# A linear-attention and ELU kernel: one batch's attention cut by heads in place of rows, and two weight matmul blocks moved ahead of a late operand

## The chip, the cores and the metric

The kernel runs on one core of one Trainium2 chip. The metric is device time in microseconds (us) of one execution; a profile's span is about 2 us shorter than that time, because it counts from the first to the last instruction. With one core there is no second die to compare with; every profiled run quoted here is at a granted TensorE clock of 0.997 to 1.0.

PE is TensorE's matrix unit (PEld its weight loads), DVE is VectorE, ACT is ScalarE, POOL is GpSimd, SP is SyncE. PSUM is the memory that PE's products go to; in these kernels a product that reuses a PSUM buffer waits until the buffer's last reader is through. A turn is a transpose on PE. An insertion is a group of small attention matmuls (64 rows) put between the full-size matmuls of a layer.

## The reference

The attention is linear (no softmax), its output is RMS-normed per head, and a two-layer network with ELU follows:

```python
# q, k, v: (8 batches, 8 heads, 576 rows, 64); w_in: 512 x 2048; w_out: 2048 x 512
kv  = einsum('bhsd,bhse->bhde', k, v)          # 64 x 64 per head, over all 576 rows
out = einsum('bhsd,bhde->bhse', q, kv)         # "scores" in the kernel
rms = sqrt(mean(out*out, axis=-1) + 1e-6)
x   = (out / rms * g_norm) -> (4608 tokens, 512)
h   = x @ w_in                                 # first layer
g   = where(h > 0, h, exp(min(h, 0)) - 1)      # ELU
y   = g @ w_out                                # second layer, float32
```

## The kernel before

The kernel works in groups T of 512 rows: group T is batch T's first 512 rows, and a ninth group collects the remaining 64 rows of all batches. The first layer has 16 output blocks f of 128 columns, done as pairs i (f = 2i, 2i+1). Each needs four matmuls, one per 128-row block c of `w_in`; a column block c of x is two heads. The second layer of a group has four output tiles j, each a sum over the 16 blocks f. The batch's attention is put between matmuls of the previous group's second layer, so that DVE and ACT work while PE goes on. PSUM has three pools that matter here: `at` (one buffer), `m1` (two buffers of two banks), `m2` (two buffers of one bank).

The three places that the change touches, in the order of time. First, the weights come in four slices, and batch 0's first six blocks f wait for one late column block of x (c = 3):

```python
edges = (0, 512, 1024, 1536, 2048)             # columns of w_in, one load per slice
...
first((0, 1, 2, 3), (0,))                      # first(fs, cs): blocks fs, rows cs
mean_first(3); log_first(3); exp_first(3); scale_first(3)    # makes x's block c = 3
first((0, 1, 2, 3), (1, 2))
for f in (0, 1, 2, 3):
    first((f,), (3,))
for f in (4, 5):
    first((f,), (0, 1, 2, 3))
... # ELU of pair 0 reads PSUM twice (exp on ACT, max on DVE), of pair 1 on ACT only
for i, parts in enumerate([[(0, 2, pair)]] + single):
    elu(0, i, parts, i == 1)()
```

Second, batch 1's attention inside batch 0's second layer. `q` turns Q, `kv` is K·V for all heads, `se` the scores, `sq`, `sum`, `inv`, `mul` the norm, and `x0`, `x1` turn x by halves of the rows:

```python
order = (2, 3, 0, 1)
for j in order: mm2_quarter(0, j, 0)           # second layer, f 0-3
at["q"]()
for j in order: mm2_quarter(0, j, 1)           # f 4-7
mm2(0, order[0], 8, 10)
at["kv"]()                                     # all 8 heads: needs the last K and V slices
for j in order[1:]: mm2(0, j, 8, 10)
at["se"]({0: None, 1: ps_m1.tile(...)})        # all heads; row half 0 in "at", 1 in "m1"
... sq0, sq1, sum0, inv0, sum1, inv1, mul0, mul1
for j in order: mm2(0, j, 10, 12)
for j in order:
    mm2(0, j, 12, FC, hold=j in (2, 3))
    ...
    if j == 0: at["x0"]()                      # turn of rows 0-255, scaled copy on ACT
```

Third, batch 1's first products, in two row halves, so that they can start with half of x; `x1` comes between:

```python
firsts = [ps_m1.tile(...) for _ in range(2)]
for cs in (slice(0, 256), slice(256, G)):
    for f in range(4):
        for c in range(KC):
            nc.tensor.matmul(firsts[f // 2][:, f % 2, cs], lhsT=w_in_sb[:, c, f*P : f*P+P],
                             rhs=xT[1](c, cs), start=(c == 0), stop=(c == KC - 1))
        if cs.start == 0 and f == 1: head_x1()  # turn of rows 256-511, scaled copy on DVE
```

## Time and profile before

The first three runs had a median of 285.66 us (285.45 to 285.68). The six that the result was compared with had 285.56 us.

| what | before |
|---|---|
| span of the profile | 283.7 us |
| PE busy | 274.4 us, 97% |
| DVE, ACT busy | 56%, 54% |
| idle PE listed by the waits | 3.7 us, of which 2.4 at start-up, all but traces of it before 47 us |

The first part of the page gives each engine's busy time, its share and its instructions:

```profile
PE 274.4 (97%) x2131; PEld 130.5 (46%) x2162; DVE 159.9 (56%) x231; ACT 153.1 (54%) x220; POOL 53.5 (19%) x94
```

PE is the bottleneck, so a gain has to come from its gaps or its work. The Trainium skill ("Trainium Kernel Development and Optimization", Performance Expectations) warns that matmul busy time is a poor measure of how close a kernel is to the limit, because matmuls are pipelined; gaps must be read from the spacing of starts, and the page's 97% hides them. PE's waits (what waited, for what, total us, times, longest):

```profile
PE bank L547 <- DVE q_two L150: 1.2, 2, 0.8
PE h_ps L607 <- DVE xT L598: 0.4, 1, 0.4
PE h_ps L802 <- ACT xT L312: 0.4, 1, 0.4
```

The first is start-up. The other two are the ones the change is about. The timeline of PE (start, duration, line, operation, count, and the recorded idle before it) shows where they stand, from batch 0's first product (14.37) to K·V of batch 2 (54.37); a full-width matmul starts every 0.216 us:

```profile
14.37 0.61 PE L607 MATMUL h_ps<-xT,w_in_sb 128*128 128x512 bf16 x2
...
16.82 0.59 PE L607 MATMUL bank<-xT,w_in_sb 128*128 128x512 bf16 x2
17.85 0.59 PE L607 MATMUL h_ps<-xT,w_in_sb 128*128 128x512 bf16 x2 [0.43 <-DVE xT L598]
...
29.07 1.24 PE L445 MATMUL o_ps<-w_out_sb,gT 128*128 128x512 bf16 x5
...
40.30 4.49 PE L445 MATMUL o_ps<-w_out_sb,gT 128*128 128x512 bf16 x19
44.83 0.62 PE L305 MATMUL at<-ident,xs 128*128 128x128 bf16 x8
45.29 1.03 PE L445 MATMUL o_ps<-w_out_sb,gT 128*128 128x512 bf16 x4
46.69 1.03 PE L802 MATMUL h_ps<-xT,w_in_sb 128*128 128x256 bf16 x8 [0.37 <-ACT xT L312]
47.55 0.61 PE L305 MATMUL at<-ident,xs 128*128 128x128 bf16 x8
48.00 2.99 PE L802 MATMUL h_ps<-xT,w_in_sb 128*128 128x256 bf16 x24
...
54.37 0.78 PE L174 MATMUL at<-v_pk,k_pk 64*64 64x64 bf16 x72
```

The two matmuls at 16.82 should be followed at 17.25; the next starts at 17.85, so 0.6 us is lost, more than the recorded 0.43, because a matmul's modelled end overlaps the next start. In the same way the four matmuls at 45.29 should be followed at 46.15, and 0.54 us is lost before 46.69. The turn at 44.83 is 0.2 us late (20 matmuls from 40.30 end at 44.62; one record is missing), and the second row half waits 0.22 us inside the line at 48.00 (the weight loads have that gap at 49.08). The three around the turn come to 0.96 us.

The chain that ended last (start, us, what) confirms that this stretch is bound by the norm on DVE and ACT, not by PE:

```profile
40.18 1.03 ACT sq L213
...
41.23 0.95 DVE ss L218
...
42.37 1.22 DVE ss L218
...
43.61 0.32 ACT ss L224
...
44.17 1.45 ACT o_sb L458 x3
45.62 1.02 ACT xT L312
...
46.69 1.03 PE h_ps L802 x8
```

Three copies of output tiles (`o_sb`) stand in this chain ahead of ACT's x copy, and the change moves them behind it.

### The profile page before, as it was taken

The numbers are of one execution on the slowest core, as the hardware profiler recorded it, in microseconds if no ns is written. First come the engines' busy times: TensorE is split into PE (matmuls) and PEld (weight loads), VectorE is DVE, ScalarE is ACT, GpSimd is POOL, SyncE is SP. The second block draws the span as 40 slices with busy tenths as digits, with TensorE's granted clock in tenths as the row PEclk, the third lists the DMA queues.
The fourth block names the chain that finished last, engine by engine and source line by source line (L and its number), as shares of the span: only waits on it lengthen the run. The fifth ranks groups of instructions, "written<-read, shape, count | busy, mean of one in ns | idle before, by whom it ended". The sixth has DMA issues, their size and how long they took to land.

```text
span 283.7 us, 5180 instructions
## 1 busy us (share of the span) xinstructions
PE 274.4 (97%) x2131; PEld 130.5 (46%) x2162; DVE 159.9 (56%) x231; ACT 153.1 (54%) x220; POOL 53.5 (19%) x94
## 2 busy tenths in 40 slices
PE   6999999999999999999999999999999999999994
PEld 2444555545544444445444444444444444444443
DVE  2359315698478636934695468544864486444400
ACT  2779535766496338634773378246923692333311
POOL 7823402251421060104210421012000000000000
PEclk9999999999999999999999999999999999999999
DMA  7999999796993598356944794355253123010122
GB/s 194 204 207 202 207 201 178 225 143 113 196 190 68 150 134 181 76 148 90 208 95 127 105 213 94 98 130 148 49 93 83 77 48 100 2 74 0 74 75 75
DMA packets 55979, 35.99 MB, mean 127 GB/s; under 512 B 32788, under 2 KB 53524, under 8 KB 55956
## 3 DMA queue, kind: packets, MB, share of 16 engines
q0 software_dynamic: 20208, 17.30, 39.7%
q1 hardware_dynamic: 35348, 17.83, 23.6%
q10 hardware_dynamic: 400, 0.52, 0.5%
q8 instruction: 17, 0.28, 0.4%
q14 instruction: 6, 0.05, 0.0%
HBM read 36.70 MB, written 9.44 MB: 163 GB/s over the span
## 4 chain that ended last, share of the span: by engine, by line
PE 90%; ACT 3%; DVE 3%; DMA 2%; issue 1%; SPq 0%
PE h_ps L398 39%; PE o_ps L445 36%; PE o_ps L858 5%; DMA st_q<-in_q_dram 2%; PE at L174 2%; PE h_ps L802 1%; DVE ss L218 1%; PE at L201 1%; PE bank L607 1%; ACT sq L213 1%; PE at L398 1%; PE bank L577 1%; PE bank L529 1%; ACT o_sb L458 1%; PE se_ps L201 1%
## 5 line engine op out<-in xcount | busy, mean ns | idle before, releaser
L398 PE MATMUL h_ps<-xT,w_in_sb 128*128 128x512 bf16 x524 | 123.6, 380 | 0.2
L445 PE MATMUL o_ps<-w_out_sb,gT 128*128 128x512 bf16 x488 | 117.9, 379 | 1.4 <-issue 0.3
L410 ACT ACTIVATE elu_e<-h_ps 128x1024 bf16<-128x1024 f32 (+1 forms) x72 | 70.8, 991 | 83.8 <-PE h_ps L398 79.2
L398 PEld LDWEIGHTS <-w_in_sb 128*128 128x128 bf16 x536 | 50.8, 98 | 61.5 <-DVE xT L333 1.7
L445 PEld LDWEIGHTS <-gT 128*128 128x128 bf16 x512 | 49.6, 98 | 59.1
L421 DVE TENSOR_SCALAR elu_e<-elu_e 128x1024 bf16<-128x1024 bf16 (+1 forms) x75 | 32.3, 431 | 70.5 <-ACT elu_e L410 70.5
L429 DVE TENSOR_TENSOR gT<-elu_e,h_ps 128x1024 bf16<-128x1024 bf16 (+1 forms) x53 | 62.6, 1181 | 5.9 <-DVE elu_e L421 0.5
L218 DVE TENSOR_REDUCE ss<-sq 128x16 f32<-128x1024 bf16 x16 | 19.3, 1218 | 13.4 <-ACT sq L213 12.7
L458 ACT COPY o_sb<-o_ps 128x512 f32<-128x512 f32 x32 | 18.5, 585 | 14.4 <-PE o_ps L445 14.4
L150 POOL COPY q_bf<-q_pk 128x512 bf16<-128x512 bf16 x24 | 14.6, 636 | 23.5 <-DMA q_pk<-in_q_dram 23.5
L416 ACT ACTIVATE elu_h<-h_ps 128x1024 bf16<-128x1024 f32 (+1 forms) x19 | 18.3, 968 | 0.0
L429 DVE TENSOR_TENSOR gT<-elu_e,elu_h 128x1024 bf16<-128x1024 bf16 x19 | 13.2, 693 | 2.9 <-ACT elu_h L416 1.7
L858 PE MATMUL o_ps<-w_out_sb,gT 128*128 128x512 bf16 (+1 forms) x79 | 14.0, 336 | 0.1
L125 POOL COPY gate<-qT 1x1 bf16<-1x1 bf16 x6 | 1.1, 179 | 59.9 <-DMA qT<-q_bf 59.9
L229 DVE TENSOR_TENSOR xs<-at,ss 128x512 bf16<-128x512 f32 x18 | 11.5, 682 | 1.2 <-ACT ss L225 1.2
L104 POOL DMA_DIRECT2D q_pk<-in_q_dram x14 | 10.5, 759 | 4.7 <-issue 1.9
L213 ACT ACTIVATE sq<-at 128x1024 bf16<-128x1024 f32 x9 | 9.4, 1044 | 2.4 <-PE at L201 2.4
L858 PEld LDWEIGHTS <-gT 128*128 128x128 bf16 x80 | 7.7, 98 | 6.4 <-DVE gT L429 0.4
L118 POOL DMA_DIRECT2D v_pk<-in_v_dram x12 | 8.4, 702 | 5.0 <-DMA w_in_sb<-in_moe_w_in_dram 2.9
L118 POOL DMA_DIRECT2D k_pk<-in_k_dram x12 | 8.3, 694 | 5.1 <-DMA w_in_sb<-in_moe_w_in_dram 3.4
L866 ACT COPY o_last<-o_ps 128x512 f32<-128x512 f32 (+1 forms) x5 | 2.5, 500 | 10.8 <-PE o_ps L858 10.8
L529 PE MATMUL bank<-zeros 128*128 128x512 bf16 x19 | 6.6, 465 | 1.4 <-DVE zeros L506 1.2
(73 smaller groups left out, 138.6 us busy)
## 6 DMA issues: line engine op xcount, KB each, us to landing
out_dram<-o_sb SPq DMA_DIRECT2D x16, 512.0 KB, 3.0
q_pk<-in_q_dram POOLq DMA_DIRECT2D x14, 256.0 KB, 5.0
k_pk<-in_k_dram POOLq DMA_DIRECT2D x6, 576.0 KB, 8.1
v_pk<-in_v_dram POOLq DMA_DIRECT2D x6, 576.0 KB, 12.2
w_in_sb<-in_moe_w_in_dram POOLq DMA_DIRECT2D x4, 512.0 KB, 10.9
w_out_sb<-in_moe_w_out_dram POOLq DMA_DIRECT2D x3, 512.0 KB, 15.5
st_q<-in_q_dram SPq DMA_DIRECT2D x2, 512.0 KB, 4.7
st_q<-in_q_dram SPq DMA_DIRECT2D x16, 64.0 KB, 2.5
```

Of the source, the lines that this page charges most:

```text
L118: nc.gpsimd.dma_start(out=raw[name, b].rearrange("p h j d -> p h (j d)")[:, hs], in_=in_[:, hs])
L150: eng.tensor_copy(out=out_, in_=in_)
L213: nc.scalar.activation(sq, se_ps, AF.Square)
L218: nc.vector.reduce_sum(out=ss, in_=sq.rearrange("p c (h e) -> p (c h) e", h=H), axis=AX.X)
L398: nc.tensor.matmul(h_ps[a][:, cs], lhsT=w_in_sb[:, c, f * P : f * P + P], rhs=x(c, cs), start=(c == 0), stop=(c == KC - 1),)
L410: nc.scalar.activation(e[:, lo:hi, :], ps, AF.Exp)
L416: nc.scalar.activation(h[:, lo:hi, :], ps, AF.Relu)
L421: nc.vector.tensor_scalar(out=e[:, lo:hi, :], in0=e[:, lo:hi, :], scalar1=1.0, scalar2=1.0, op0=ALU.min, op1=ALU.subtract,)
L429: nc.vector.tensor_tensor(out=gT[T][:, 2 * i + lo : 2 * i + hi, :], in0=e[:, lo:hi, :], in1=h, op=ALU.add if relu else ALU.max,)
L445: nc.tensor.matmul(o_ps[T, j], lhsT=gT[T][:, f, j * P : j * P + P], rhs=w_out_sb[:, f, :], start=(f == 0), stop=(f == FC - 1),)
L458: nc.scalar.copy(o_sb[T][:, j % 2, :], o_ps.pop((T, j)))
L858: nc.tensor.matmul(ps, lhsT=gT[B][:, f, j * P : j * P + P], rhs=w_out_sb[:, f, cols], start=(f == 0), stop=(f == FC - 1),)
```

## The change

The intent: start batch 1's norm earlier by doing half of the heads as soon as the first halves of K and V are there, so that x is ready when PE asks; and fill batch 0's gap with blocks f 4 and 5, for which the second `w_in` slice is made narrower. The core of the diff (the new pieces `kvu`, `seu`, `mulu`, `xu` do for heads of pair index u what `kv`, `se`, `mul`, `x` did for all heads or a row half; their bodies are cut):

```diff
-    edges = (0, 512, 1024, 1536, 2048)
+    edges = (0, 512, 768, 1280, 1664, 2048)
...
-    for f in (0, 1, 2, 3):
-        first((f,), (3,))
-    for f in (4, 5):
-        first((f,), (0, 1, 2, 3))
+    first((4, 5), (0, 1, 2))
+    first((0, 1, 2, 3, 4, 5), (3,))
...
-    (the order of batch 1's attention shown above)
+    scores = ps_m1.tile([P, 2, G], FP32, name="se_ps", tag="mm1")
+    for j in range(J):
+        mm2_quarter(0, j, 0)
+        if j == 2: at["q"]()
+    for j in range(J):
+        mm2_quarter(0, j, 1)
+        if j == 1: at["kvu0"]()
+        if j == 2: at["seu0"](scores); at["sq0"](); at["sum0"]()
+    for j in range(J):
+        mm2(0, j, 8, 10)
+        if j == 1: at["kvu1"](); at["inv0"](); at["mulu0"]()
+    at["seu1"](); at["sq1"](); at["sum1"]()
+    for j in range(J):
+        mm2(0, j, 10, 12)
+        if j == 1: at["inv1"](); at["xu0"](scores[:, 0, :])
+    at["mulu1"]()
+    for j in range(J):
+        mm2(0, j, 12, FC, hold=j > 1)
+        if j == 2: at["xu1"](scores[:, 1, :])
...
-    (batch 1's first products in two row halves, head_x1 between)
     for i in range(8):
-        if i < 2: elu(1, i, [(0, 2, firsts[i])], i == 0)()
-        else: mm1(1, i, relu=i == 4, home="m2" if i in (2, 5) else "m1")()
+        mm1(1, i, relu=i in (1, 4), home={0: "at", 2: "m2", 5: "m2"}.get(i, "m1"))()
```

More of the change, by code (lines that the diff above doesn't have):

```diff
@@ L355, in kv_out, with kv_u, se_u, scores @@
             )
-        def kv_part(u):
+        def kv_u(u):
             def product():
-                kv_half(u)()
+                st["kv"] = at_tile(FP32).rearrange("p (s x) -> p s x", s=2)
+                kv_single(T, st["kv"], u)
                 kv_out(slice(u, u + 1))
             return product
+        def se_u(u):
+            def scores(home=None):
+                if home is None:
+                    home = at_tile(FP32).rearrange("p (l f) -> p l f", l=2)
+                for j in range(J):
+                    for s in range(2):
+                        for l in range(2):
+                            ls = slice(l * 64, l * 64 + 64)
+                            nc.tensor.matmul(
+                                home[:, l, (2 * j + s) * D : (2 * j + s + 1) * D],
+                                lhsT=st["qT"](2 * s + u, j)[ls, :],
+                                rhs=kv_sb[ls, T, 2 * s + u, :],
+                                start=True,
+                                stop=True,
+                            )
+                st["se", u] = home
+            return scores
@@ new lines, in scale_u, with scale @@
+        def scale_u(u):
+            def scale():
+                if u == 0:
+                    st["xs"] = attp.tile([P, J, DM], BF16, name="xs", tag="xs")
+                se, ss = st.pop(("se", u)), st.pop(("ss", u))
+                for l in range(2):
+                    c = 2 * u + l
+                    nc.vector.tensor_tensor(
+                        out=st["xs"][:, :, c * P : c * P + P].rearrange(
+                            "p j (s e) -> p j s e", s=2
+                        ),
+                        in0=se[:, l, :].rearrange("p (j s e) -> p j s e", s=2, e=D),
+                        in1=ss[:, 8 * l : 8 * l + 8]
+                        .rearrange("p (j s) -> p j s", s=2)
+                        .to_broadcast([P, J, 2, D]),
+                        op=ALU.mult,
+                    )
+            return scale
@@ new lines, in x_u, with turn @@
+        def x_u(u, eng):
+            def turn(ps):
+                if u == 0:
+                    st["x"] = attp.tile([P, KC, G], BF16, name="xT", tag="xT")
+                    xT[T] = lambda c, cs: st["x"][:, c, cs]
+                xt = ps.bitcast(BF16).rearrange("p (c t) -> p c t", c=2)
+                for n in range(2):
+                    c = 2 * u + n
+                    for j in range(J):
+                        nc.tensor.transpose(
+                            xt[:, n, j * P : j * P + P],
+                            st["xs"][:, j, c * P : c * P + P],
+                            ident,
+                        )
+                x = st["x"][:, 2 * u : 2 * u + 2, :]
+                if eng is nc.scalar:
+                    nc.scalar.mul(x, xt, g_col)
+                else:
+                    nc.vector.tensor_scalar(
+                        out=x, in0=xt, scalar1=g_col, scalar2=None, op0=ALU.mult
+                    )
+            return turn
@@ L366, in attention @@
         for h in range(2):
-            pieces[f"kv{h}"] = kv_part(h)
+            pieces[f"kvu{h}"] = kv_u(h)
+            pieces[f"seu{h}"] = se_u(h)
+            pieces[f"mulu{h}"] = scale_u(h)
+            pieces[f"xu{h}"] = x_u(h, (nc.scalar, nc.vector)[h])
             pieces[f"x{h}"] = x_t(h, (nc.scalar, nc.vector)[h])
@@ L707 @@
         o_ps[0, 2 + a] = both[:, a, :]
-    order = (2, 3, 0, 1)
-    for j in order:
+    scores = ps_m1.tile([P, 2, G], FP32, name="se_ps", tag="mm1")
+    for j in range(J):
         mm2_quarter(0, j, 0)
-    at["q"]()
-    for j in order:
+        if j == 2:
+            at["q"]()
+    for j in range(J):
         mm2_quarter(0, j, 1)
-    mm2(0, order[0], 8, 10)
-    at["kv"]()
-    for j in order[1:]:
-        mm2(0, j, 8, 10)
-    at["se"]({0: None, 1: ps_m1.tile([P, 2, G], FP32, name="se_ps", tag="mm1")})
-    for n in range(2):
-        at[f"sq{n}"]()
-    for n in range(2):
-        at[f"sum{n}"]()
-        at[f"inv{n}"]()
-    at["mul0"]()
-    at["mul1"]()
-    for j in order:
+        if j == 1:
+            at["kvu0"]()
+        if j == 2:
+            at["seu0"](scores)
+            at["sq0"]()
+            at["sum0"]()
+    for j in range(J):
+        mm2(0, j, 8, 10)
+        if j == 1:
+            at["kvu1"]()
+            at["inv0"]()
+            at["mulu0"]()
+    at["seu1"]()
+    at["sq1"]()
+    at["sum1"]()
+    for j in range(J):
         mm2(0, j, 10, 12)
+        if j == 1:
+            at["inv1"]()
+            at["xu0"](scores[:, 0, :])
+    at["mulu1"]()
     unpack_q(2, Q)
     ahead["qd"]()
-    for j in order:
-        mm2(0, j, 12, FC, hold=j in (2, 3))
-        if j == 3:
-            mm2_out(0, 2)
-            mm2_out(0, 3)
-        if j == 0:
-            at["x0"]()
+    for j in range(J):
+        mm2(0, j, 12, FC, hold=j > 1)
+        if j == 2:
+            at["xu1"](scores[:, 1, :])
+    mm2_out(0, 2)
+    mm2_out(0, 3)
     def fetch(b):
@@ L793 @@
     fetch(3)
-    head_x1 = at["x1"]
     at, ahead = ahead, attention(3)
     ahead["qd"]()
-    gT[1] = mlpg.tile([P, FC, G], BF16, name="gT", tag="gT")
-    firsts = [ps_m1.tile([P, 2, G], FP32, name="h_ps", tag="mm1") for _ in range(2)]
-    for cs in (slice(0, 256), slice(256, G)):
-        for f in range(4):
-            for c in range(KC):
-                nc.tensor.matmul(
-                    firsts[f // 2][:, f % 2, cs],
-                    lhsT=w_in_sb[:, c, f * P : f * P + P],
-                    rhs=xT[1](c, cs),
-                    start=(c == 0),
-                    stop=(c == KC - 1),
-                )
-            if cs.start == 0 and f == 1:
-                head_x1()
     for i in range(8):
-        if i < 2:
-            elu(1, i, [(0, 2, firsts[i])], i == 0)()
-        else:
-            mm1(1, i, relu=i == 4, home="m2" if i in (2, 5) else "m1")()
+        mm1(1, i, relu=i in (1, 4), home={0: "at", 2: "m2", 5: "m2"}.get(i, "m1"))()
         if i == 3:
```

## The prediction

> **What bounds the kernel.** TensorE. The page has PE busy 97% of 283.7 us at full clock, and 90% of the chain that ended last. The view of waits lists about 3.5 us of idle PE, nearly all before 47 us; after that the timeline has matmuls end to end. Only gaps or work of PE in the first 51 us can pay, and what is won there should carry to the end.
>
> **Where PE stands still there (timeline of PE and weight loads).**
> - Batch 0's first products stop 0.6 us before 17.85 us, for the last x0 block (DVE; recorded as 0.43).
> - Batch 1's turn starts at 44.83 us, about 0.2 us late for DVE's scaling.
> - After it, 0.54 us (recorded 0.37) until 46.69 us, for ScalarE's x copy.
> - The second row half waits 0.22 us at 49.08 us for DVE's x copy.
> The last three: 0.96 us.
>
> **What the change does.**
> 1. Batch 0: six matmuls (f 4,5) move ahead of the late x0 block and fill the 0.6 us. The narrower second w_in slice must land by about 17.25 us; slices now land at about 14.3 and 17.9, so 256 columns should by about 16.6. But the first ELU starts 0.7 us later (18.48 to about 19.17). Its PSUM pair is freed by exp 1.02 + DVE 0.43 + 1.22, at about 22.0 us; product pair i=4 would want it at 21.57. A new stall of about 0.45 us: net 0.15.
> 2. Batch 1 by halves of heads: square 1.02, sum 1.22, Ln/Exp 0.55, scale 1.28, turn, copy 0.75 to 1.14 start about 3 us earlier for the first half, with second-layer matmuls between. I trace x's first half ready at about 44.5 us and the second at 46.5, before PE asks (46.5 and 47.0): all 0.96 us goes, perhaps 0.1 to 0.2 stays at the first turn.
> 3. Cost: K·V and scores are each inserted twice. An insertion of small matmuls costs about 0.13 us beyond its own work (kv: 0.81 against 0.67; the weight loads idle 0.42 before each). Two more: +0.3 us.
> 4. 32 matmuls of 256 columns become 16 of 512. The Trainium skill ("TensorE: Matmul & The Clock Gate", back-to-back issue gap) gives N/2.4 + 2.5 ns, so 109 and 216 ns; the trace agrees (0.108 and 0.216 us). The wider form itself saves nothing.
> 5. One more w_in issue (0.75 us of POOL) is harmless: loads are queued 12 to 18 us ahead of landing. K and V halves land at about 33.6 and 37.7 us, w_out's last slices at 39.0 and 41.5; the new order uses them at about 35.2, 38.7, 40.5 and 42.6.
>
> **Sum.** 0.15 + 0.96 − 0.3 − 0.1 = 0.7 us. Predicted 284.95 us, 284.3 to 285.5 holding 8 in 10. Faster by over 2%: 0.5%; within 2%: 99%; slower: 0.5%.
>
> **What would show it.** PE's waits for x0 (L598 of before) and x copies (L312, L314) vanish; a wait of 0.3 to 0.5 us for DVE's gT appears before i=4 near 21.6 us; batch 0's second layer starts at about 28.9 us (29.07 before); batch 1's first product at about 46.5 without a wait; batch 2's K·V at about 53.6 instead of 54.37; from there every stage is 0.7 us earlier. PE's busy time rises by up to 0.2 us.
>
> **What would make it wrong.** The 256-column slice or columns from 768 landing late (stall at 17.3 or 19.8 us); the "at" buffer not free for the first K·V half (35.2 us, I expect 34.7); the first half's chain longer than traced; no stall at i=4 (gain up to 1.1 us); DMA moved by the earlier PE.

## The result, and the profile after

| | before | after |
|---|---|---|
| median | 285.56 us (285.36 to 285.71, 6 runs) | 284.97 us (284.88 to 285.09, 6 runs) |
| ratio | | 0.998, 95% interval 0.9967 to 0.9993 |
| span of the profile | 283.7 us | 283.3 us |

A ratio here is the mean time of one kernel's fast runs over the mean time of the other's fast runs of the same rounds, so it is not quite the ratio of the medians quoted. The kernel is faster by 0.6 us; by a threshold of 2% it is the same.

The page's first part and PE's waits after the change:

```profile
PE 277.0 (98%) x2146; PEld 129.2 (46%) x2146; DVE 159.6 (56%) x231; ACT 153.4 (54%) x221; POOL 54.3 (19%) x95
...
PE h_ps L465 <- DVE gT L496: 0.3, 1, 0.3
```

Both waits for x are gone, and a new one for DVE's `gT` has come. (PE's busy time rose by 2.6 us although 16 matmuls fewer are issued. The instruction counts show that the first trace misses records: 2131 matmuls beside 2162 weight loads, where the second has 2146 of each; busy time is no check on this scale.) PE's timeline:

```profile
14.54 0.60 PE L674 MATMUL h_ps<-xT,w_in_sb 128*128 128x512 bf16 x2
...
20.04 1.89 PE L465 MATMUL h_ps<-xT,w_in_sb 128*128 128x512 bf16 x8
22.23 3.61 PE L465 MATMUL h_ps<-xT,w_in_sb 128*128 128x512 bf16 x16 [0.31 <-DVE gT L496]
...
29.14 2.75 PE L512 MATMUL o_ps<-w_out_sb,gT 128*128 128x512 bf16 x12
...
35.53 0.48 PE L174 MATMUL at<-v_pk,k_pk 64*64 64x64 bf16 x36
35.94 1.04 PE L512 MATMUL o_ps<-w_out_sb,gT 128*128 128x512 bf16 x4
36.91 0.41 PE L373 MATMUL se_ps<-kv_sb,qT 64*128 64x64 bf16 x16
37.25 1.90 PE L512 MATMUL o_ps<-w_out_sb,gT 128*128 128x512 bf16 x8
39.08 0.48 PE L174 MATMUL at<-v_pk,k_pk 64*64 64x64 bf16 x36
...
41.72 0.61 PE L413 MATMUL se_ps<-ident,xs 128*128 128x128 bf16 x8
...
46.06 1.03 PE L512 MATMUL o_ps<-w_out_sb,gT 128*128 128x512 bf16 x4
46.92 1.89 PE L465 MATMUL at<-xT,w_in_sb 128*128 128x512 bf16 x8
...
53.92 0.78 PE L174 MATMUL at<-v_pk,k_pk 64*64 64x64 bf16 x72
```

At 22.23 the product pair i=4 comes 0.46 us late (20.04 + 8 × 0.216 = 21.77). It writes the PSUM banks of batch 0's first pair. DVE's last read of them is the second of these instructions (start, duration), until about 22.2 us; the first of them starts when ACT's exp, begun at 19.37 us (18.48 before), is through:

```profile
20.43 0.43 DVE L488 TENSOR_SCALAR elu_e<-elu_e 128x1024 bf16<-128x1024 bf16 x1 [2.46 <-ACT elu_e L477]
20.96 1.22 DVE L496 TENSOR_TENSOR gT<-elu_e,h_ps 128x1024 bf16<-128x1024 bf16 x1
```

From 35.5 us on, second-layer matmuls and attention follow one another without a listed wait: the first product of batch 1 follows the last four matmuls at exactly 46.06 + 0.86 us, and the chain of this stretch is now PE alone.

```profile
42.33 3.45 PE o_ps L512 x16
45.78 0.45 PE se_ps L413 x8
46.23 0.86 PE o_ps L512 x4
```

The account, in times that start at batch 0's first product (14.37 us before, 14.54 after), because the loads ahead of it move it by up to 0.35 us from run to run:

| from the first product to | before | after | difference |
|---|---|---|---|
| batch 0's second layer | 14.70 | 14.60 | −0.10 |
| batch 2's K·V | 40.00 | 39.38 | −0.62 |

So batch 0 gave 0.10 us (0.56 won until i=3, which starts 5.50 us after the first product in place of 6.06; 0.46 lost again at i=4), and batch 1 gave 0.52 us. The second is the 0.96 us of waits less a cost: the timeline spaces K·V's insertion at 0.81 us before and 2 × 0.51 after, that of the scores at 0.68 before and 2 × 0.45 after, so 0.43 us more. 0.96 − 0.43 = 0.53. Put otherwise, cutting an insertion in two costs its fixed part once more: 2 × 0.51 − 0.81 = 0.21 us for K·V and 2 × 0.45 − 0.68 = 0.22 us for the scores.

The diff holds more than the account names: another order of the output tiles j, the output copies moved, and another PSUM home and relu choice for batch 1's first ELUs. None of these was run alone; the account, which closes to 0.01 us, leaves little room for them.

### The profile page after: what moved, and what is told of

Its sections match the earlier page's. It is cut to its first block, busy times and chain, and to the rows that moved or that the text cites. A ratio compares the mean times of both kernels' runs of the same rounds, so it can differ in the third digit from the quotient of the medians.

```text
span 283.3 us, 5185 instructions
## 1 busy us (share of the span) xinstructions
PE 277.0 (98%) x2146; PEld 129.2 (46%) x2146; DVE 159.6 (56%) x231; ACT 153.4 (54%) x221; POOL 54.3 (19%) x95
## 4 chain that ended last, share of the span: by engine, by line
PE 95%; DMA 2%; DVE 1%; ACT 0%; issue 0%; SPq 0%; DVEq 0%
PE h_ps L465 41%; PE o_ps L512 39%; PE o_ps L912 5%; DMA st_q<-in_q_dram 2%; PE at L174 2%; PE at L465 1%; PE at L201 1%; PE bank L674 1%; PE h_ps L674 1%; PE bank L596 1%; PE bank L644 1%; PE se_ps L201 1%; DVE gT L496 0%; PE kv_ps L174 0%; ACT elu_e L477 0%; PE at L185 0%
## 5 line engine op out<-in xcount | busy, mean ns | idle before, releaser
L465 PE MATMUL h_ps<-xT,w_in_sb 128*128 128x512 bf16 x536 | 125.8, 379 | 0.3 <-DVE gT L496 0.3
L512 PE MATMUL o_ps<-w_out_sb,gT 128*128 128x512 bf16 x512 | 120.5, 379 | 0.0
L477 ACT ACTIVATE elu_e<-h_ps 128x1024 bf16<-128x1024 f32 (+1 forms) x71 | 70.0, 995 | 81.8 <-PE h_ps L465 79.6
L465 PEld LDWEIGHTS <-w_in_sb 128*128 128x128 bf16 x552 | 52.5, 98 | 64.1 <-DVE xT L333 1.7
L496 DVE TENSOR_TENSOR gT<-elu_e,h_ps 128x1024 bf16<-128x1024 bf16 (+1 forms) x52 | 61.4, 1180 | 5.8 <-DVE elu_e L488 0.5
L229 DVE TENSOR_TENSOR xs<-at,ss 128x512 bf16<-128x512 f32 x16 | 10.2, 682 | 1.2 <-ACT ss L225 1.2
L596 PE MATMUL bank<-zeros 128*128 128x512 bf16 x20 | 7.4, 495 | 1.2 <-DVE zeros L573 1.2
```

The source lines that it names most:

```text
L465: nc.tensor.matmul(h_ps[a][:, cs], lhsT=w_in_sb[:, c, f * P : f * P + P], rhs=x(c, cs), start=(c == 0), stop=(c == KC - 1),)
L477: nc.scalar.activation(e[:, lo:hi, :], ps, AF.Exp)
L496: nc.vector.tensor_tensor(out=gT[T][:, 2 * i + lo : 2 * i + hi, :], in0=e[:, lo:hi, :], in1=h, op=ALU.add if relu else ALU.max,)
L512: nc.tensor.matmul(o_ps[T, j], lhsT=gT[T][:, f, j * P : j * P + P], rhs=w_out_sb[:, f, :], start=(f == 0), stop=(f == FC - 1),)
```

## The experiments

All gave a right result. "Trace" is the change, against the kernel before, of the time from the first product to batch 2's K·V, in one profiled run each; the two kernels that were traced twice repeat within 0.04 us (after −0.62 and e10 −0.61, e3 −1.12 and e11 −1.08). Times are medians of 5 runs (6 for e8); those of the kernel before belong to the same chip.

| run | time | before, same chip | ratio (95% interval) | trace |
|---|---|---|---|---|
| e1_head_only | 285.54 | 285.68 | 0.9994 (0.9981 to 1.0007) | −0.01 |
| e2_att_only | 285.06 | 285.68 | 0.9976 (0.9963 to 0.9988) | −0.52 |
| e3_short_fill | 284.58 | 285.68 | 0.9959 (0.9946 to 0.9971) | −1.12 |
| e4_relu_first | 285.43 | 285.68 | 0.9989 (0.9975 to 1.0002) | −0.24 |
| e5_old_slices | 285.46 | 285.47 | 0.9994 (0.9981 to 1.0008) | +0.15 |
| e6_late_half | 285.71 | 285.47 | 1.0008 (0.9995 to 1.002) | +0.13 |
| e7_wide_only | 286.30 | 285.47 | 1.0034 (1.0022 to 1.0047) | +0.86 |
| e8_wide_own | 286.15 | 285.69 | 1.0019 (1.0006 to 1.0033) | +0.25 |
| e9_head_short | 285.49 | 285.69 | 0.9994 (0.9982 to 1.0006) | −0.06 |
| e10_after_again | 284.88 | 285.68 | 0.9979 (0.9966 to 0.9993) | −0.61 |
| e11_short_again | 284.42 | 285.68 | 0.9957 (0.9944 to 0.9969) | −1.08 |

### e1 and e2: each part alone

e1 is the kernel before with the first two hunks of the diff; e2 is the kernel after without them.

> The kernel before with only the batch 0 part of the change (five w_in slices, f 4 and 5 ahead of the late x0 block). Theory A (the gap at 17.85 us is filled, but the first ELU starts 0.65 us later and frees its PSUM pair later, so the product pair i=4 waits about 0.45 us): gains 0.1 us at i=4, about 285.45 us. Rival R1 (the filled gap carries to the end): gains 0.6 us, about 284.95. Batch 1's stalls (0.2, 0.54, 0.22 us) stay as they were.

> The kernel after with the batch 0 part undone. Theory A (nearly all the gain is batch 1's stalls, 0.96 us, less about 0.43 us for two more insertions of small matmuls): 0.5 us faster than before, about 285.05; the wait at x0 (0.4 to 0.6 us) is back and no wait at i=4. Rival R1 (half or more of the gain is batch 0's): 0.0 to 0.3 us faster.

e2 came out as expected: without batch 0's part nearly the whole gain is there. e1 gained 0.14 us by the median, with an interval that includes no gain at all, and its waits show the trade: the wait for x0 is gone, the one for `gT` has come, and batch 1's is as it was.

```profile
PE h_ps L800 <- ACT xT L312: 0.4, 1, 0.4
PE h_ps L398 <- DVE gT L429: 0.3, 1, 0.3
```

In e1's trace the second layer started 0.18 us earlier than before, counted from the first product, but K·V of batch 2 only 0.01 us: the undivided K·V of batch 1 took 0.88 us until the next matmul (37.55 to 38.43) in place of 0.71 (37.62 to 38.33, with one missing record put back). Its last V slice landed at about 38.0 us (issued at 25.80, 12.2 us to landing), in the middle of it. e9 returns to this.

### e3 and e4: what the wait at i=4 is for

e3 puts three of the six matmuls ahead of the late block and three behind; e4 keeps the order of after and lets ACT, not DVE, read the first pair last.

```diff
e3, against after
-    first((4, 5), (0, 1, 2))
-    first((0, 1, 2, 3, 4, 5), (3,))
+    first((4, 5), (0,))
+    first((4,), (1,))
+    first((0, 1, 2, 3), (3,))
+    first((5,), (1,))
+    first((4, 5), (2, 3))

e4, against after
-        elu(0, i, parts, i == 1)()
+        elu(0, i, parts, i < 2)()
```

> The kernel after, but only three of the six matmuls of f 4,5 stand ahead of the late x0 block, the other three behind f 0 to 3. The work is the same. Theory A: three matmuls (0.65 us) still fill the gap, the first ELU starts 0.65 us earlier, the pair is free at about 21.5 us and i=4 starts unhindered: another 0.45 us, about 284.5 us. Rival R2 (the wait at i=4 is not due to the first ELU's time, or what is won there is lost again at the next PSUM wait or DMA): under 0.15 us against after.

> The kernel after with the first ELU's max taken from a ScalarE relu copy in place of PSUM, so that ScalarE frees the pair, not VectorE. Theory A: the pair is free at 19.37+1.02+0.95 = 21.3 us, before i=4 asks at 21.77: the stall of 0.46 us goes; ScalarE is 0.95 us later after that, so i=5 (its PSUM is freed by relus) may wait about 0 to 0.3 us. Time 284.5 to 284.9. Rival R2 (the wait is for something else, such as a w_in slice): the stall at i=4 stays and the time is that of after.

e3's PE never waits after start-up. Three matmuls are enough filler (block c=3 is there when they end), and i=3 to i=5 run as one piece:

```profile
17.00 1.24 PE L674 MATMUL bank<-xT,w_in_sb 128*128 128x512 bf16 x5
18.08 0.59 PE L674 MATMUL h_ps<-xT,w_in_sb 128*128 128x512 bf16 x2
...
20.02 5.34 PE L465 MATMUL h_ps<-xT,w_in_sb 128*128 128x512 bf16 x24
```

In e4 the wait at i=4 is gone too, as theory A says, with the order untouched. So the wait was for DVE's read of the first pair. But the time was missed: expected 284.5 to 284.9, measured 285.43, because a larger wait has come at i=6, which takes the `at` banks:

```profile
PE at L465 <- DVE gT L496: 0.7, 1, 0.7
```

ACT did 0.9 us more work ahead of the later ELUs, DVE came later to the pair f 4,5, and i=6 started 0.84 us late (at 26.02 in place of 25.18). I had looked at i=5 alone.

### e5: the narrower slice

The kernel after with `edges = (0, 512, 1024, 1536, 2048)`.

> The kernel after with the four w_in slices of before (512 columns each). Theory A: f 4 then waits for the second slice, which landed at about 17.9 us in before: PE waits 0.4 to 0.8 us at about 17.3 us, the first ELU and all that hangs on it (i=4) come as much later: 0.4 to 0.8 us slower than after, about 285.5. Rival R3 (the narrower slice is not needed): same as after.

```profile
PE h_ps L465 <- DVE gT L496: 0.6, 1, 0.6
PE bank L674 <- DMA w_in_sb<-in_moe_w_in_dram: 0.4, 1, 0.4
```

PE waited for the slice until 17.68 us, and the wait at i=4 grew behind it. All of the change's gain was gone: by the trace, the batch 0 order without the slice (+0.15) is worse than no batch 0 part at all (e2, −0.52).

### e6: the first half of the heads, but later

Work and insertions as in after; only the place differs.

```diff
     for j in range(J):
         mm2_quarter(0, j, 1)
-        if j == 1: at["kvu0"]()
-        if j == 2: at["seu0"](scores); ...
+        if j == 2: at["kvu0"]()
+        if j == 3: at["seu0"](scores); ...
```

> The kernel after with the first half's K.V and scores each put four second-layer matmuls (0.86 us) later; the work and the number of insertions are the same. Theory A (the gain is the early start of the first half's chain, and its slack at the first turn is about zero: scaling ended at 41.67, the turn began at 41.72): the turn waits about 0.85 us and the time is 0.8 us over after, about 285.8, worse than before. Rival R4 (the halves by heads pay by themselves, by turning all rows of a column block at once): under 0.2 us over after.

```profile
PE se_ps L413 <- DVE xs L391: 0.6, 1, 0.6
```

The first turn waited (42.18 us in place of 41.37, so 0.81 us), and the time was 0.24 us over before by the medians, where after was 0.6 under it. 0.86 us of delay cost about 0.8 us: the start of the chain had next to no slack, and the cut by heads pays only through the early start. With this delay the gain is gone; whether it is a loss against before is not shown (1.0008, interval 0.9995 to 1.002; trace +0.13).

### e7 and e8: the wide products alone

The kernel before with batch 1's first products at 512 columns: the block with `firsts` is replaced by `head_x1()` and a plain loop `mm1(1, i, relu=i in (0, 4), ...)`. e8 differs from e7 in the PSUM tile of the second turn:

```diff
-    at["se"]({0: None, 1: ps_m1.tile([P, 2, G], FP32, name="se_ps", tag="mm1")})
+    se_home = ps_m1.tile([P, 2, G], FP32, name="se_ps", tag="mm1")
+    at["se"]({0: None, 1: se_home})
...
-    head_x1()
+    head_x1(se_home[:, 0, :])
```

> The kernel before with batch 1's first products as 512 columns at once, the second turn ahead of them. Theory A (256 and 512 columns cost the same per column, the halves only hid a wait): the first product waits until about 47.45 us for VectorE's x copy and then takes 3.45 us; 0.1 us slower than before, about 285.65. Rival R5 (half as many matmuls and weight loads are the gain): 0.3 to 0.6 us faster than before.

> The run e7_wide_only came out 0.8 us slower than before, not 0.1: its second turn waited for ScalarE's copy of the first turn's half of the same PSUM tile (0.37 us recorded, at 46.55 us) and VectorE's copy after it. Here the second turn goes to another PSUM tile (the freed scores tile), nothing else changes. Theory A: the turn runs at about 46.0 us, VectorE's copy ends at about 47.3, 16 matmuls of 512 columns end at about 50.8 us as the 32 of 256 did: the time is that of before within 0.2 us. Rival R5 (wide matmuls cost or save something by themselves): 0.4 us or more away from before, either way.

e7 was 0.83 us slower, not 0.1. PE's waits show two links where I had counted one:

```profile
PE h_ps L398 <- DVE xT L314: 0.9, 1, 0.9
...
PE at L305 <- ACT xT L312: 0.4, 1, 0.4
```

The second turn wrote one half of the tile whose other half ACT was still copying, and waited for it. With another tile (e8) this wait is gone and the turn follows at once:

```profile
46.29 0.61 PE L305 MATMUL se_ps<-ident,xs 128*128 128x128 bf16 x8
47.75 7.08 PE L398 MATMUL h_ps<-xT,w_in_sb 128*128 128x512 bf16 x32 [0.85 <-DVE xT L314]
```

By the trace e8 is 0.25 us over before, just outside the 0.2 expected. Its times are not settled: 285.63 to 286.76 us, about three times as wide as those of most runs (e7's, 286.21 to 287.28, are as wide), with a median 0.46 us over before, which is what the rival asked for. So the time of e8 decides nothing finer than "no gain". What decides against the rival is the spacing: 32 wide matmuls and the change-over to K·V take 7.01 us in e8 (so at most 0.219 each), and the eight of 256 columns at 46.69 in before take 0.86 us (0.108 each), so two of those cost one of these. The wide form alone gains nothing; without a wait it is only possible when x is ready in time. Why the times of e7 and e8 scatter, and so whether something later in e8 costs time, stays open.

### e9: batch 0's mended order without the batch 1 part

The kernel before with the slices of after and the order of e3.

> The kernel before with the mended batch 0 order of e3_short_fill and none of the batch 1 part. Theory B (batch 0's gain cannot be kept without the batch 1 part, because the undivided K.V of batch 1 then comes to the last V slice, which lands at about 38.0 us, whatever PE does): the second layer starts 0.6 us earlier, K.V starts at about 37.1 and waits about 0.5 us in its middle; the time is 0.0 to 0.25 us under before. Rival R6 (the two parts add up): 0.5 to 0.6 us under before.

```profile
28.47 3.62 PE L445 MATMUL o_ps<-w_out_sb,gT 128*128 128x512 bf16 x16
...
37.02 0.48 PE L174 MATMUL at<-v_pk,k_pk 64*64 64x64 bf16 x36
37.84 0.48 PE L174 MATMUL at<-v_pk,k_pk 64*64 64x64 bf16 x36 [0.34 <-DMA v_pk<-in_v_dram]
```

The second layer starts 0.57 us earlier than before, counted from the first product. Then K·V stops in its middle for the last V slice (it takes 1.22 us until the next matmul, 37.02 to 38.24, in place of 0.71), and after it all but 0.06 us is gone. The two parts do not add up: batch 0's gain lasts only with K·V cut in two, whose second half comes to V at 38.6 us (e3), after the slice has landed (at about 38.1 us there). e2, e3 and e9 together show it: −0.52 and −0.06 alone, −1.12 together.

### e10 and e11: after and the mended order on one chip

> The kernel after once more, beside e11 on one chip, so that the mended order is compared with it directly. Theory A: 0.5 to 0.7 us under before.

> The kernel of e3_short_fill once more on the same chip. Theory A: 0.35 to 0.55 us under e10_after_again, 1.0 to 1.2 under before. Rival: the difference between e3 and after was one of chips, and is under 0.15 us here.

The mended order is 0.46 us under after and 1.26 us under before by the medians (0.9957). The second lies just outside the 1.0 to 1.2 expected, and so does e10's 0.80 by the medians (0.5 to 0.7 expected); by the ratios, which are of means, e10 is 0.6 under and e11 1.2. The ratio to before agrees with that of e3. The version of e3 is thus the best of all; the same work in another order of six matmuls adds 0.46 us to the gain (0.47 by the trace).

## Why the prediction was right or wrong

It said 284.95 us; 284.97 was measured. A hit within 0.02 us is partly luck: the 0.7 us were taken off the 285.66 of the first three runs, and against the 285.56 of all six the gain was 0.59. The mechanism held: the waits that it named went and the new one came where it was foreseen. One term of its sum was mis-sized (point 3). Point by point:

1. **Batch 0: right, with its new wait.** Net 0.15 us predicted, 0.10 measured; the wait at i=4 was predicted at 0.45 us and is 0.46 by the spacing. e3 and e4 show that it is for the first pair's PSUM. What I did not see is that the same six matmuls in another order avoid it, and (e9) that even the full batch 0 gain would have been lost without the batch 1 part.
2. **Batch 1's waits: right.** All 0.96 us went. The 0.1 kept back for the first turn was not needed, but e6 shows the turn has almost no slack. The second half of x had less room than predicted: its copy ended at 47.09 us (46.5 predicted), and PE asked for it at about 47.35, the third matmul from 46.92.
3. **The cost of insertions: mis-sized.** I took 0.3 us for two more; it was 0.43. An insertion does cost about 0.15 us beyond its own work, as taken. But half the matmuls do not take half the time: the weight loads of K·V take 0.67 us for 72 and 0.37 for 36, those of the scores 0.52 for 32 and 0.29 for 16. The Trainium skill ("TensorEngine Tiling (Array Packing)", Key Properties) says that changing the tiling mode drains the engine. The traces fit that on the way in: the weight loads idle 0.42 us before every such insertion. That the drain is the fixed part of the cost is not shown.
4. **The wide form: right**, by the spacing of starts (e7, e8), which also fits the skill's figures that the prediction names ("TensorE: Matmul & The Clock Gate", Back-to-back issue gap: 109 and 216 ns; here 108 and 216). The section gives them for an isolated matmul; what it says of a stream does not fit (see the end).
5. **Loads: right, with less room than thought.** K·V's halves and the last slices were in time. The narrower slice is needed (e5).
6. **Checks.** Second layer at 29.14 (28.9 predicted), first product at 46.92 (46.5), K·V of batch 2 at 53.92 (53.6): each a little late, 0.17 us of it because the first product started that much later. The check on PE's busy time was wrong: it rose by 2.6 us, not 0.2, for missing records.

The sum, 0.15 + 0.96 − 0.3 − 0.1 = 0.7, was in the trace 0.10 + 0.96 − 0.43 = 0.63: the 0.13 us missing in the cost of insertions were nearly covered by the 0.1 kept back for the first turn, which is luck too.

## What to carry to other kernels

On an engine that is busy 97% of the time, read gaps from the spacing of starts, and ask of every filler what it delays: here the filler held back the first ELU, and with it a PSUM buffer that was asked for 2.4 us after that ELU began. Use only as much filler as the gap needs. Cutting a dependent chain in two paid here by its early start alone, cost a fixed sum for each further insertion (about 0.21 us), and may be what lets an earlier gain pass a late load; so test the parts of a change alone and together.

## What the Trainium skill lacked or had wrong

- "TensorEngine Tiling (Array Packing)", Key Properties, names the drain at a change of tiling mode but gives no cost. Here an insertion of 64-row matmuls between full-array ones cost about 0.14 us (36 of K·V: 0.51 us against 0.37 of weight loads) to 0.16 us (16 of the scores: 0.45 against 0.29) beyond its weight loads, which idle 0.42 us before it; cutting one insertion into two cost 0.21 to 0.22 us.
- "TensorE: Matmul & The Clock Gate", Back-to-back issue gap, puts a stream of weight loads and matmuls in a real kernel at about 131 ns per matmul of 512 columns and says that its formula (216 ns) over-counts there. Here such streams ran at 216 ns: 24 matmuls of e3, each with its weight load, took 5.18 us (20.02 to the next start at 25.20).
- "Trainium Kernel Development and Optimization", Performance Expectations, is right about matmul busy time. It lacks that records can be missing: PE's busy time rose from 274.4 to 277.0 us while 16 matmuls fewer were issued and the kernel got faster.
- No page that I read tells how late a load queued behind others lands when it is cut smaller. Here the POOL issues that waited for the `w_in` slices came at 14.61 and 18.17 us with 512 columns, and at 14.78 and 17.14 us with 256 in the second: half the data came 2.36 us after the first slice in place of 3.56, not in half the time. The DMA view puts its landing at about 16.8 (issued at 7.9, landed 8.9 us later). I had estimated a landing by 16.6; PE asked at 17.45, so about 0.6 us were to spare.
